# A pre-norm SSM convolution and MLP block on one core: the gate and the norms rewritten, the tail put in order by repeated list schedules

## The chip, the core and the metric

The kernel runs on one NeuronCore of a Trainium2 chip. The core has a matrix engine (TensorE, PE in the profile, with PEld for its weight loads), a vector engine (VectorE, DVE), a scalar engine (ScalarE, ACT), GpSimd (POOL) and a queue engine for transfers (SyncE, SP). Each engine works through its own instructions in the order in which the program issued them and waits on semaphores for the others. The metric is the device time of one execution in microseconds; the profile shows one execution, instruction by instruction.

## What is computed

A sequence of 2048 positions with 512 features, in bfloat16. Part A is a gated long convolution: k is convolved with four taps, multiplied by v, convolved causally over the whole sequence with a per-feature kernel by Fourier transforms, and the result y gates the normalized input. Part B is a normalization, a mixer that shifts features by one or two positions between two matrix products, and an MLP of width 1792.

```python
x = A_q
h = x + _A_ref(_layernorm(x, axis=-1), A_k, A_v, A_shift_k, A_ssm_k, A_ssm_D)   # _A_ref ends in: return q * y
h2 = h + _B_ref(_layernorm(h, axis=-1), B_w1, B_w2, B_w3, B_w4)
...
def _B_ref(x, w1, w2, w3, w4):
    h = _gelu(_layernorm(x, axis=-1) @ w1)
    c = D // 4
    g0 = jnp.pad(h[:, :, 0*c:1*c], ((0, 0), (1, 0), (0, 0)))[:, :S, :]
    ...
    hs = jnp.concatenate([g0, g1, g2, g3], axis=-1) @ w2
    x1 = x + hs
    h2 = _gelu(_layernorm(x1, axis=-1) @ w3) @ w4
    return x1 + h2
```

So h is normalized twice in a row: once to make the input of part B, hn, and that once more ahead of w1. Both are a scale and a shift of h by row.

## The kernel before

The 2048 positions are kept as 16 blocks of 128 rows (position 16p + b lies in partition p of block b), each 128 x 512. The program has three parts.

*The forward transforms* (lines 171 to 414) load k, v, q and the convolution kernel, make tables, transform both factors, and collect mean and variance of each row of q (qstat, lines 361 to 364). qnorm (line 366) turns these into qrs = 1/std and qnm = -mean/std.

*The inverse stage* (lines 418 to 451) loops over 16 frequency blocks. fwd (line 418) does the last transform step on TensorE (step2, line 340, which reads tables in rf), copies it on ScalarE, and forms two products with the kernel's spectrum on VectorE (lines 423 and 424). inv (line 428) transforms back, evacuates PSUM on ScalarE or VectorE by a running count of load (evac, line 282), and stores the block through an SP transfer into wv (line 438), a re-layout that the last transform step reads. Beside the second half of this loop GpSimd computes qn = (q-mean)/std for the 16 blocks (line 450). The loop's end, line 452, is followed by the loads of w1 and w2 on GpSimd's queue (lines 465 and 466, into rf) and of w3 and w4 on SP's (467 and 468).

*The tail* (lines 471 to 705) is written as tasks: each has a name, engines it may run on with a price in microseconds, a function that issues its instructions, tasks it depends on, a buffer pool it takes a slot of, and a task whose buffer it is the last to read. Plan.emit (line 54) makes a list schedule: among all tasks that could run it takes the one with the earliest start, ties going to the longest path behind it (tail), then issues all in order of start. This fixes the order on every engine. The tasks are, for a block b or a pair p of blocks:

- I: the last inverse step for four blocks (32 matmuls, line 503), into four of six PSUM slots ("mm").
- Y: ScalarE copies y to bfloat16 (yb). H, on VectorE: y times qn, plus q gives h; mean and variance of h (hsum, lines 521 to 524).
- rr, on GpSimd: scales and shifts of both normalizations of a pair, with a power of -1/2 (hnorm, lines 530 to 541; line 528 is the power).
- hb: h scaled for w1, on ScalarE or VectorE (lines 548, 550). N, on GpSimd: hn = normalized h (line 556).
- LT and TE: transposes on TensorE (line 563) and copies out of PSUM (lines 483, 485). W: product with w1 for a pair (line 577). U: gelu on ScalarE (line 583).
- X: product with w2 on shifted blocks (line 602); it needs the gelus of the block's neighbours up to two blocks away. S, on VectorE: x1 = X + hn and its statistics (lines 611 to 613).
- r1, on GpSimd: 1/std of x1 (lines 619 and 528). lb: x1 normalized, on VectorE (line 626). L and E: transposes and copies. R, on GpSimd: the residual x1 + h (line 632).
- For four groups of four blocks, M: product with w3 (14 tasks of four matmuls, line 639), G: gelu (line 645), O: product with w4 (four tasks of 14 matmuls, line 654), Z: add the residual and store (lines 662 and 663).

The first group is blocks 2 to 5, since blocks 0 and 1 come last in the mixer's order. M of group g waits for O of group g - 2. In the profile of the page a name such as rd or rc is a large buffer that several stages share.

Of the kernel before, what the change touches and what calls it, by code (L numbers as in the profile page):

```python
# [3 lines left out]

# [6 lines left out]
P = 128  # L11
S = 2048
D = 512
F = 1792
NB = S // P
DC = D // P
FC = F // P
L = 2 * S
# [15 lines left out]
class Plan:  # L34
# [4 lines left out]

    LAT = 0.2  # L40

    def __init__(self, pools):
        self.pools, self.t = pools, []

    def add(self, opts, fn, deps=(), take=None, drop=None, rank=0.0):
        t = dict(opts=opts, fn=fn, deps=[d for d in deps if d is not None], take=take, drop=drop, rank=rank, n=len(self.t),
                 left=0, out=[], done=None)
        if drop is not None:
            t["deps"] = t["deps"] + [drop]
            drop["left"] += 1  # L50
        self.t.append(t)
        return t

    def emit(self):
        for t in self.t:
            for d in t["deps"]:
                d["out"].append(t)
        for t in reversed(self.t):
            t["tail"] = t["rank"] + min(t["opts"].values()) + max((o["tail"] + self.LAT for o in t["out"]), default=0.0)
        held = {p: [] for p in self.pools}  # L60
        free = {e: 0.0 for t in self.t for e in t["opts"]}
        wait, order = list(self.t), []
        while wait:
            best = None
            for t in wait:
                if any(d["done"] is None for d in t["deps"]):
                    continue
                at = max((d["done"] + (0.0 if t["opts"].keys() == {d["eng"]} else self.LAT) for d in t["deps"]), default=0.0)
                if t["take"]:
                    h, k = held[t["take"]], self.pools[t["take"]]  # L70
                    if len(h) >= k:
                        if h[-k]["free"] is None:
                            continue
                        at = max(at, h[-k]["free"] + self.LAT)
                for e, c in t["opts"].items():
                    key = (max(at, free[e]), -t["tail"], c, t["n"])
                    if best is None or key < best[0]:
                        best = key, t, e, c
            (at, *_), t, e, c = best
            t["eng"], t["done"], t["free"] = e, at + c, None  # L80
            free[e] = at + c
            if t["take"]:
                held[t["take"]].append(t)
# [648 lines left out]
```

## Time and profile before

| | |
|---|---|
| Median of three runs | 277.77 us (275.23 to 278.82) |
| The profiled execution | 275.51 us, of it 273.7 us span |
| Mean granted TensorE clock | 0.961 |
| HBM traffic | 11.02 MB read, 2.10 MB written |
| Forward transforms, up to about | 76 us |
| Inverse stage | 76 to 110 us |
| Tail | 110 to 273.7 us |

The span is the time from the first to the last instruction recorded; the execution's own time has 1.8 us more around it. A group row of the profile gives line, engine, operation, output <- input, shape and count, then total busy time and the mean of one in nanoseconds, then the idle time just before these instructions and what ended it. A timeline row gives start, length, engine, line. The chain of waits follows the work back from the last instruction, at each step to what released it.

### The profile page before, as it was taken

How to read it: one execution, taken by the hardware profiler on the slowest of the kernel's cores; microseconds unless marked ns; L12 is line 12 of the kernel's file. 1: busy time of each engine (PE TensorE's matmuls, PEld its weight loads, DVE VectorE, ACT ScalarE, POOL GpSimd, SP SyncE). 2: the span in 40 equal slices, each digit the busy share in tenths (PEclk: the TensorE clock that was granted, in tenths of full speed). 3: DMA queues.
4: the chain of work that ended last, by engine and by line, in shares of the span. 5: the costliest groups of instructions: out<-in, count | busy, mean ns of one | idle time of the engine just before them, and what ended most of it. 6: DMA issues, size and time to landing. Idle time of an engine off the chain costs nothing.

```text
span 273.7 us, 4566 instructions
## 1 busy us (share of the span) xinstructions
PE 234.7 (86%) x1791; PEld 118.1 (43%) x1803; DVE 158.8 (58%) x296; ACT 145.2 (53%) x207; POOL 89.1 (33%) x148
## 2 busy tenths in 40 slices
PE   8666959999399976739878988999999989999994
PEld 4522835664132321214664654444444454444441
DVE  7986736689568996699996999920122240002222
ACT  3628245978679973468983444666300066660000
POOL 4503000000500599688999795840000000000000
PEclk9999997999779999795999999999999999999999
DMA  7999983033303433990000000000011100000111
GB/s 246 251 293 366 377 312 156 2 156 153 154 2 134 175 147 142 357 353 2 2 0 0 2 1 0 2 0 0 0 41 58 38 19 2 0 0 19 54 44 38
DMA packets 18791, 28.08 MB, mean 103 GB/s; under 512 B 10065, under 2 KB 13906, under 8 KB 17234
## 3 DMA queue, kind: packets, MB, share of 16 engines
q1 hardware_dynamic: 17952, 26.74, 28.0%
q0 software_dynamic: 288, 1.05, 0.9%
q8 instruction: 14, 0.23, 0.4%
q10 hardware_dynamic: 530, 0.01, 0.1%
q14 instruction: 7, 0.06, 0.1%
HBM read 11.02 MB, written 2.10 MB: 48 GB/s over the span
## 4 chain that ended last, share of the span: by engine, by line
PE 50%; DVE 23%; POOL 11%; DMA 6%; issue 4%; ACT 4%; SPq 2%; ACTq 0%; DVEq 0%; POOLq 0%
PE mm L654 18%; PE mm L639 17%; POOL rd L556 4%; PE pk L354 4%; DVE st L612 3%; POOL rr L528 3%; DMA rd<-rc 3%; DVE q_sb L611 3%; DVE vst L290 2%; DMA q_sb<-in_A_q_dram 2%; SPq L301 2%; DVE rt L263 2%; PE psg L344 2%; DVE pr L423 2%; PE psk L344 2%
## 5 line engine op out<-in xcount | busy, mean ns | idle before, releaser
L662 DVE TENSOR_TENSOR ob<-mm,rd 128x512 bf16<-128x512 f32 x16 | 11.1, 692 | 76.6 <-PE mm L654 76.6
L639 PE MATMUL mm<-rc,rb 128*128 128x512 bf16 x219 | 48.7, 379 | 1.3 <-DVE q_sb L611 1.0
L654 PE MATMUL mm<-rt,ra 128*128 128x512 bf16 x220 | 48.5, 379 | 0.2
L645 ACT ACTIVATE ra<-mm 128x512 bf16<-128x512 f32 x56 | 33.4, 597 | 19.5 <-PE mm L639 19.5
L639 PEld LDWEIGHTS <-rb 128*128 128x128 bf16 x224 | 21.8, 98 | 27.4 <-issue 1.8
L654 PEld LDWEIGHTS <-ra 128*128 128x128 bf16 x224 | 21.9, 98 | 26.4
L483 ACT COPY rc<-ptx 128x512 bf16<-128x512 bf16 x28 | 15.4, 589 | 32.0 <-PE ptx L563 31.8
L450 POOL TENSOR_SCALAR rd<-q_sb,qrs,qnm 128x512 bf16<-128x512 bf16 x16 | 18.8, 1188 | 18.0 <-DVE pr L424 18.0
L354 PE MATMUL pk<-diag,rb 128*128 128x128 bf16 x256 | 19.0, 232 | 3.0 <-DVE xk L357 2.9
L354 PEld LDWEIGHTS <-rb 128*128 128x128 bf16 x256 | 17.6, 150 | 7.4 <-issue 6.1
L563 PE MATMUL ptx<-ident,hb 128*128 128x128 bf16 x128 | 12.1, 224 | 8.6 <-ACT hb L548 5.1
L632 POOL TENSOR_TENSOR rd<-q_sb,rd 128x512 bf16<-128x512 bf16 x16 | 18.3, 1158 | 1.2 <-DVE q_sb L611 1.2
L577 PE MATMUL mm<-rc,rf 128*128 128x256 bf16 x128 | 16.0, 280 | 0.6 <-ACT rb L583 0.4
L287 ACT CAST asb<-psk 128x1024 bf16<-128x1024 f32 x16 | 16.1, 1030 | 0.5 <-ACT asb L287 0.4
L602 PE MATMUL mm<-rf,rb 128*128 128x512 bf16 x61 | 15.2, 380 | 1.4 <-ACT rb L583 1.0
L503 PE MATMUL mm<-ra,f_71 32*128 32x512 bf16 x128 | 12.3, 490 | 2.9 <-DMA ra<-vst 1.9
L563 PEld LDWEIGHTS <-hb 128*128 128x128 bf16 x128 | 8.7, 99 | 13.7 <-ACT hb L548 6.5
L367 POOL TENSOR_SCALAR qrs<-qmv 128x16 f32<-128x16 f32 x1 | 0.2, 204 | 43.8 <-DVE qmv L363 43.8
L357 DVE TENSOR_TENSOR xk<-pk,rb 128x512 bf16<-128x512 f32 x16 | 10.9, 681 | 5.5 <-PE pk L354 5.5
L577 PEld LDWEIGHTS <-rf 128*128 128x128 bf16 x128 | 12.5, 100 | 3.3 <-issue 1.7
L362 DVE BATCH_NORM_STATS2 qst<-q_sb 128x6 f32<-128x512 bf16 x16 | 10.9, 680 | 5.1 <-DMA q_sb<-in_A_q_dram 5.1
L344 PE MATMUL psg<-rd,rf 128*64 128x512 bf16 x64 | 10.3, 418 | 4.1 <-ACT rd L287 4.0
(213 smaller groups left out, 375.4 us busy)
## 6 DMA issues: line engine op xcount, KB each, us to landing
rd<-rc SPq DMA_DIRECT2D x16, 256.0 KB, 5.0
rc<-ra SPq DMA_DIRECT2D x16, 256.0 KB, 2.4
ra<-vst SPq DMA_DIRECT2D x16, 256.0 KB, 2.4
ra<-in_A_ssm_k_dram SPq DMA_DIRECT2D x4, 512.0 KB, 5.1
rb<-in_A_v_dram SPq DMA_DIRECT2D x2, 1024.0 KB, 8.3
q_sb<-in_A_q_dram SPq DMA_DIRECT2D x2, 1024.0 KB, 6.7
out_dram<-ob SPq DMA_DIRECT2D x16, 128.0 KB, 1.8
rb<-in_B_w_dram SPq DMA_DIRECT2D x1, 1792.0 KB, 7.7
```

The source lines that it names most:

```text
L287: nc.scalar.copy(o, i)
L344: nc.tensor.matmul(ps[64 * t:64 * t + 64, r, :], lhsT=ftab[:, kh, r, t, :], rhs=z[:, kh, t, :], start=True, stop=True)
L354: nc.tensor.matmul(pk[:, c * P:(c + 1) * P], lhsT=kT[:, c, 16 + b - j:KW - 16 + b - j + 1:16], rhs=diag[:, c, j, :], start=(j == 0), stop= ...
L450: nc.gpsimd.tensor_scalar(out=qn[:, b, :], in0=q_sb[:, b, :], scalar1=qrs[:, b:b + 1], scalar2=qnm[:, b:b + 1], op0=MUL, op1=ADD)
L483: nc.scalar.copy(o, i)
L563: nc.tensor.transpose(pt[:, c, :], tl[key][:, c * P:(c + 1) * P], ident[:])
L577: nc.tensor.matmul(pw_[:, j * 256:(j + 1) * 256], lhsT=w1_sb[:, k, m * P:(m + 1) * P], rhs=hnT[:, k, p * 256:(p + 1) * 256], start=(k == 0 ...
L602: nc.tensor.matmul(px[:], lhsT=shifted(m, b), rhs=w2_sb[:, m, :], start=(m == 0), stop=(m == DC - 1))
L632: nc.gpsimd.tensor_tensor(out=xh1[:, b, :], in0=x1[:, b, :], in1=h_sb[:, b, :], op=ADD)
L639: nc.tensor.matmul(pg[:], lhsT=w3_sb[:, k, fc * P:(fc + 1) * P], rhs=lnT[:, k, g * 512:(g + 1) * 512], start=(k == 0), stop=(k == DC - 1))
L645: nc.scalar.activation(gbuf[:, g % 2, fc, :], tl["g", g, fc][:], ACT.Gelu_apprx_tanh)
L654: nc.tensor.matmul(po[:], lhsT=gbuf[:, g % 2, fc, i * P:(i + 1) * P], rhs=w4_sb[:, fc, :], start=(fc == 0), stop=(fc == FC - 1))
```

## The change

The new kernel computes the same function.

- Plan is rewritten. `forward` is a list schedule as before (earliest start, then a priority, where the engine is chosen by earliest finish). `backward` takes the engines of a forward schedule and schedules the tasks from the end, one after another on each engine, which gives each a latest start; these are the priorities of the next forward schedule. `solve` does this 40 times, with random disturbances every sixth time, and keeps the order whose planned end is earliest. A task may take several slots at once (`many`), and the slots are freed one by one (`part`).
- qn, qnm and their GpSimd passes are gone. y is gated as h = (q - mean) * (1 + y/std): ScalarE makes z = 1 + y*qrs in float32 (`gate`), VectorE makes (q - mean) * z. The stored h lacks the row mean of q, which the residual adds back. (The two normalizations do not see a constant added to a row.)
- hn is no longer computed. hb, the normalized input of w1, is kept for all 16 blocks in rd, and x1 is hb * cr + X, where cr, the ratio of the two scales (tasks `cr`), turns the second normalization back into the first.
- The variance-plus-epsilon and the negated mean move from GpSimd to VectorE (`uw`, `ux`); GpSimd keeps the powers and the small products. The scale-and-shift passes hb and lb are both in the form multiply, add, and may run on VectorE, GpSimd or ScalarE.
- The residual R moves from GpSimd to VectorE and now also waits for the last M of its group.
- A dummy gelu after the inverse stage loads ScalarE's table there. The pools yb (4) and hb (5) go; z (4) and lb (6) come. Prices in the tasks are changed, and M, O and E get ranks for the first forward schedule.

```diff
+    def forward(self, prio):
...
+            for n in ready:
+                t, at0 = ts[n], 0.0
...
+                at0 = {e: max([at0, free[e]] + [done[d] + (0.0 if eng[d] == e else self.LAT) for d in t["deps"]]) for e in t["opts"]}
+                e = min(at0, key=lambda e: (at0[e] + t["opts"][e], t["opts"][e]))
+                key = (at0[e], -prio[n], n)
+                if best is None or key < best[0]:
...
+            (at, *_), n, e, c = best
+            t = ts[n]
+            done[n], eng[n] = at + c, e
             free[e] = at + c
...
+            order.append((at, n))
+        return max(done.values()), order, done, eng
+
+    def backward(self, done, eng):
...
+        while ready:
+            best = None
+            for n in ready:
+                e = eng[n]
+                at = max([free[e]] + [left[o] + (0.0 if eng[o] == e else self.LAT) for o in ts[n]["out"]])
+                key = (at, -done[n], n)
+                if best is None or key < best[0]:
+                    best = key, n, e
+            (at, *_), n, e = best
+            left[n] = free[e] = at + ts[n]["opts"][e]
+            ready.remove(n)
...
+        return left
...
+    def solve(self):
+        tail, best, rnd = {}, None, random.Random(1)
+        for t in reversed(self.t):
+            tail[t["n"]] = t["rank"] + min(t["opts"].values()) + max((tail[o] + self.LAT for o in t["out"]), default=0.0)
+        prio = top = tail
+        for i in range(self.rounds):
+            r = self.forward(prio)
+            if r is not None and (best is None or r[0] < best[0]):
+                best, top = r, prio
+            if r is None or i % 6 == 5:
+                prio = {n: p + rnd.gauss(0.0, 3.0) for n, p in top.items()}
+            else:
+                prio = self.backward(r[2], r[3])
+        return best
+
+    def emit(self):
+        best = self.solve()
+        for _, n in sorted(best[1]):
+            self.t[n]["fn"](best[3][n])
+        return best[0]
...
-        nc.gpsimd.tensor_tensor(out=qnm[:], in0=qmv[:, :, 0], in1=qrs[:], op=MUL)
-        nc.gpsimd.tensor_scalar(out=qnm[:], in0=qnm[:], scalar1=-1.0, scalar2=0.0, op0=MUL, op1=ADD)
...
-    qn = view(rd, NB * D, NB * D, "p (b d) -> p b d", b=NB)
...
-        if i >= NH // 2 + 1:
-            for b in range(2 * (i - NH // 2 - 1), min(NB, 2 * (i - NH // 2))):
-                nc.gpsimd.tensor_scalar(out=qn[:, b, :], in0=q_sb[:, b, :], scalar1=qrs[:, b:b + 1], scalar2=qnm[:, b:b + 1],
-                                        op0=MUL, op1=ADD)
...
+    nc.scalar.activation(dum[:], negpi[:], ACT.Gelu_apprx_tanh)
...
-    hn, xh1, x1 = qn, qn, q_sb
+    hbm = view(rd, NB * D, NB * D, "p (b d) -> p b d", b=NB)
+    xh1, x1 = hbm, q_sb
...
     nc.gpsimd.memset(h1T[:, :, :, XW - 1:XW], 0.0)
-    plan = Plan({"mm": 6, "pt": 2, "yb": 4, "hb": 5})
...
-    def ycopy(b):
-        def f(e):
-            yb = tl["yb", b] = lnp.tile([P, D], BF16, name="yb", tag="yb", bufs=4)
-            copy(e, yb[:], tl["y", b][:])
-        return f
+    def inv1(bl):
...
+    def gate(b):
+        def f(e):
+            z = tl["z", b] = lnp.tile([P, D], F32, name="z", tag="z", bufs=4)
+            nc.scalar.activation(z[:], tl["y", b][:], ACT.Identity, bias=1.0, scale=qrs[:, b:b + 1])
+        return f
+
+    def stats(name, b, src):
+        mv = pair(name, b // 2, 2, 2, bufs=8)
+        st = stp.tile([P, 6], F32, name="st", tag="st")
+        nc.vector.bn_stats(st[:], src)
+        nc.vector.bn_aggr(mv[:, b % 2, :], st[:])
...
     def hsum(b):
         def f(e):
...
-            nc.vector.tensor_tensor(out=ty[:], in0=tl["yb", b][:], in1=qn[:, b, :], op=MUL)
-            nc.vector.tensor_tensor(out=h_sb[:, b, :], in0=ty[:], in1=q_sb[:, b, :], op=ADD)
-            nc.vector.bn_stats(st[:], h_sb[:, b, :])
-            nc.vector.bn_aggr(mv[:, i, :], st[:])
-        return f
-
-    def power(dst, n):
-        nc.gpsimd.tensor_tensor(out=dst, in0=dst, in1=mhalf[:, 0:n], op=OP.pow)
+            nc.vector.scalar_tensor_tensor(out=h_sb[:, b, :], in0=q_sb[:, b, :], scalar=qmv[:, b, 0:1], in1=tl["z", b][:],
+                                           op0=SUB, op1=MUL)
+            stats("hv", b, h_sb[:, b, :])
+        return f
...
+    def negmean(p, n, mv):
+        nm = pair(n, p, 2, bufs=8)
+        nc.vector.tensor_scalar(out=nm[:], in0=mv[:, :, 0], scalar1=-1.0, scalar2=None, op0=MUL)
+
...
+    def hvar(p):
...
+            uw = pair("uw", p, 2, 2, bufs=8)
+            for a, (m_, e_) in enumerate(((1.0, EPS), (1.0 + EPS, EPS * EPS))):
+                nc.vector.tensor_scalar(out=uw[:, a, :], in0=tl["hv", p][:, :, 1], scalar1=m_, scalar2=e_, op0=MUL, op1=ADD)
+            negmean(p, "hm", tl["hv", p])
+        return f
...
     def hnorm(p):
         def f(e):
...
-            for a, (m_, e_) in ((1, (1.0 + 1e-5, 1e-10)), (0, (1.0, 1e-5))):
-                nc.gpsimd.tensor_scalar(out=rr[:, a, :], in0=mv[:, :, 1], scalar1=m_, scalar2=e_, op0=MUL, op1=ADD)
-            power(rr[:].rearrange("p a i -> p (a i)"), 4)
-            for a in range(2):
-                nc.gpsimd.tensor_tensor(out=nm[:, a, :], in0=mv[:, :, 0], in1=rr[:, a, :], op=MUL)
-            nc.gpsimd.tensor_scalar(out=nm[:], in0=nm[:], scalar1=-1.0, scalar2=0.0, op0=MUL, op1=ADD)
-        return f
+            uw, rr, nm = tl["uw", p], pair("rr", p, 2, 2, bufs=8), tl["hm", p]
+            power(rr[:].rearrange("p a i -> p (a i)"), uw[:].rearrange("p a i -> p (a i)"), 4)
+            nc.gpsimd.tensor_tensor(out=nm[:], in0=nm[:], in1=rr[:, 1, :], op=MUL)
+        return f
...
+    def hback(p):
...
+            uw, rr, cr = tl["uw", p], tl["rr", p], pair("cr", p, 2, bufs=8)
+            nc.gpsimd.tensor_tensor(out=cr[:], in0=uw[:, 1, :], in1=rr[:, 1, :], op=MUL)
+            nc.gpsimd.tensor_tensor(out=cr[:], in0=cr[:], in1=rr[:, 0, :], op=MUL)
+        return f
...
+    def scaled(e, o, i, sc, bi):
+        if e == "A":
+            nc.scalar.activation(o, i, ACT.Identity, bias=bi, scale=sc)
+        else:
+            (nc.gpsimd if e == "G" else nc.vector).tensor_scalar(out=o, in0=i, scalar1=sc, scalar2=bi, op0=MUL, op1=ADD)
...
     def hbf(b):
         def f(e):
...
-    def hnf(b):
...
-            nc.gpsimd.tensor_scalar(out=hn[:, b, :], in0=h_sb[:, b, :], scalar1=sc, scalar2=bi, op0=MUL, op1=ADD)
+            tl["hb", b] = hbm[:, b, :]
+            scaled(e, hbm[:, b, :], h_sb[:, b, :], tl["rr", b // 2][:, 1, b % 2:b % 2 + 1], tl["hm", b // 2][:, b % 2:b % 2 + 1])
...
     def x1sum(b):
         def f(e):
...
-            nc.vector.tensor_tensor(out=x1[:, b, :], in0=tl["x", b][:], in1=hn[:, b, :], op=ADD)
-            nc.vector.bn_stats(st[:], x1[:, b, :])
-            nc.vector.bn_aggr(tl["mv2", b // 2][:, i, :], st[:])
+            nc.vector.scalar_tensor_tensor(out=x1[:, b, :], in0=hbm[:, b, :], scalar=tl["cr", b // 2][:, b % 2:b % 2 + 1],
+                                           in1=tl["x", b][:], op0=MUL, op1=ADD)
+            stats("xv", b, x1[:, b, :])
...
+    def xvar(p):
...
+            nc.vector.tensor_scalar(out=pair("r1", p, 2)[:], in0=tl["xv", p][:, :, 1], scalar1=1.0, scalar2=EPS, op0=MUL, op1=ADD)
+            negmean(p, "xm", tl["xv", p])
...
     def x1norm(p):
         def f(e):
...
+            power(r1[:], r1[:], 2)
+            nc.gpsimd.tensor_tensor(out=nm[:], in0=nm[:], in1=r1[:], op=MUL)
...
     def lbf(b):
         def f(e):
...
-            nc.vector.tensor_scalar(out=hb[:], in0=x1[:, b, :], scalar1=tl["mv2", b // 2][:, b % 2, 0:1],
-                                    scalar2=tl["r1", b // 2][:, b % 2:b % 2 + 1], op0=SUB, op1=MUL)
...
+            scaled(e, lb[:], x1[:, b, :], tl["r1", b // 2][:, b % 2:b % 2 + 1], tl["xm", b // 2][:, b % 2:b % 2 + 1])
...
     def resid(b):
         def f(e):
-            nc.gpsimd.tensor_tensor(out=xh1[:, b, :], in0=x1[:, b, :], in1=h_sb[:, b, :], op=ADD)
+            nc.vector.scalar_tensor_tensor(out=xh1[:, b, :], in0=x1[:, b, :], scalar=qmv[:, b, 0:1], in1=h_sb[:, b, :],
+                                           op0=ADD, op1=ADD)
...
-            for i in range(4):
-                task(("I", b + i), {"PE": 2.2 * (i == 3)}, inv1(b + i), [("I", b + i - 1)] if b + i else [], take="mm")
-        task(("Y", b), {"A": 0.6}, ycopy(b), [("I", b | 3)], take="yb", drop=("I", b))
-        task(("H", b), {"V": 1.75}, hsum(b), drop=("Y", b))
+            task(("I", b // 4), {"PE": 2.45}, inv1(b // 4), take="mm", many=4)
+        task(("Y", b), {"A": 0.72}, gate(b), take="z", drop=("I", b // 4), part=b % 4)
+        task(("H", b), {"V": 1.6}, hsum(b), drop=("Y", b))
...
-            task(("rr", p), {"G": 2.0}, hnorm(p), [("H", b - 1), ("H", b)])
+            task(("uw", p), {"V": 0.24}, hvar(p), [("H", b - 1), ("H", b)])
+            task(("rr", p), {"G": 1.35}, hnorm(p), [("uw", p)])
+            task(("cr", p), {"G": 0.55}, hback(p), [("rr", p)])
...
-                task(("hb", c), {"A": 0.68, "V": 0.42}, hbf(c), [("rr", p)], take="hb")
...
+                task(("hb", c), {"V": 0.42, "G": 0.92, "A": 0.8}, hbf(c), [("rr", p)])
...
-            for c in (b - 1, b):
-                task(("N", c), {"G": 0.9}, hnf(c), [("rr", p)])
...
-        task(("S", b), {"V": 1.6}, x1sum(b), [("N", b)], drop=("X", b))
+        task(("S", b), {"V": 1.6}, x1sum(b), [("cr", b // 2)], drop=("X", b))
...
-            task(("r1", p), {"G": 1.2}, x1norm(p), [("S", b - 1), ("S", b)])
+            task(("ux", p), {"V": 0.17}, xvar(p), [("S", b - 1), ("S", b)])
+            task(("r1", p), {"G": 1.05}, x1norm(p), [("ux", p)])
...
-                task(("lb", c), {"V": 0.42}, lbf(c), [("r1", p)], take="hb")
+                task(("lb", c), {"V": 0.42, "G": 0.92, "A": 0.8}, lbf(c), [("r1", p)], take="lb")
...
-                task(("R", c), {"G": 1.2}, resid(c), [("S", c)])
+                task(("E", c), {"A": 0.6, "V": 0.42}, tcopy(("lb", c), lnT, order.index(c)), drop=("L", c),
+                     rank=400.0 - 20.0 * (order.index(c) // 2))
...
-                 take="mm")
...
+                 take="mm", rank=100.0 - 20.0 * g)
...
+        for b in bs:
+            task(("R", b), {"V": 0.76}, resid(b), [("S", b), ("M", g, FC - 1)])
...
```

153 lines of the change are left out of this document (70 added, 83 removed).

## The prediction

> **What bounds the kernel now.** I read the page first, then each stage by windows, then the chain of work, then groups and timeline.
>
> ```profile
> span 273.7 us, 4566 instructions
> PE 234.7 (86%) x1791; PEld 118.1 (43%) x1803; DVE 158.8 (58%) x296; ACT 145.2 (53%) x207; POOL 89.1 (33%) x148
> ```
>
> TensorE is busiest, but that share is a mean over unlike stages. The windows cut the planned tail (lines 471 to 705) at its turning points. After the two times and the length come PE, PEld, DVE, ACT and POOL busy, granted clock, DMA share and GB/s.
>
> ```profile
> 110.38:141.20 30.82, 23.32 (x220) 13.50 (x221) 27.81 (x61) 23.70 (x42) 26.05 (x54) 0.83 0.41 152
> 141.20:172.02 30.82, 26.55 (x179) 15.43 (x181) 27.61 (x56) 15.21 (x29) 24.74 (x38) 1.00 0.00 1
> 172.02:218.80 46.78, 46.57 (x215) 21.28 (x219) 12.52 (x23) 15.66 (x27) 8.27 (x10) 1.00 0.06 20
> 218.80:221.50 2.70, 1.93 (x25) 1.44 (x23) 2.44 (x6) 1.64 (x3) 0.00 (x0) 1.00 0.14 49
> 221.50:270.36 48.86, 48.53 (x227) 22.16 (x230) 5.70 (x11) 17.20 (x29) 0.00 (x0) 1.00 0.06 19
> sum 159.98, PE 146.90 PEld 73.80 DVE 76.09 ACT 73.41 POOL 59.06; mean PE 29.38 PEld 14.76 DVE 15.22 ACT 14.68 POOL 11.81
> ```
>
> From 172.02 TensorE is full. In the 61.6 us before that, VectorE is busy 55.4 and GpSimd 50.8, TensorE only 49.9. Over the tail TensorE idles 159.98 - 146.90 = 13.1 us, 11.8 of it before 172.02. That idle time is what another order can win. The chain (start, length, what) says who holds TensorE back:
>
> ```profile
> 118.25 1.69 POOL rd L556 x2
> ...
> 122.53 1.69 POOL rd L556 x2
> ...
> 145.31 1.02 POOL rr L528
> ...
> 171.40 0.59 DVE q_sb L611
> 172.02 7.50 PE mm L639 x34
> ```
>
> Up to 147 GpSimd's norm work sets the pace, 122.53 - 118.25 = 4.28 us for a pair of blocks; then VectorE's x1 sums (line 611) hold it to 172. The first feed-forward matmuls (M, line 639) come at the end of all that, though the first group of them needs only four x1 blocks.
>
> **The change, part by part.**
>
> *Before the tail.* The sixteen (q-mean)/std passes of line 450 leave GpSimd. Groups of the products in the inverse stage from 76 to 92.2, without those passes, and from 92.2 to 107.5, beside them; the last row is that second window:
>
> ```profile
> L423 DVE TENSOR_TENSOR pr<-asb,rd 128x1024 bf16<-128x1024 bf16 x9 | 6.2, 688 | 2.8 <-ACT asb L287 2.8
> ...
> L423 DVE TENSOR_TENSOR pr<-asb,rd 128x1024 bf16<-128x1024 bf16 x7 | 5.9, 846 | 0.1
> L424 DVE TENSOR_TENSOR pr<-asb,rd 128x1024 bf16<-128x1024 bf16 x7 | 5.6, 798 | 0.0
> ...
> 92.20:107.50 15.30, 11.50 (x88) 3.50 (x90) 14.54 (x18) 11.04 (x12) 15.25 (x12) 1.00 0.36 135
> ```
>
> VectorE is the bound there (14.54 of 15.30), and its products grew by 7 x (0.846 - 0.688) + 7 x (0.798 - 0.688) = 1.9 us. This comes back: **-1.9 us** on the path (other end 0, if ScalarE's evacuations become the bound at once). The two small operations that made qnm go too; nothing waits for GpSimd there, so they are worth nothing.
>
> *Weights.* On GpSimd's queue the w1 and w2 loads stood behind line 450.
>
> ```profile
> 101.25 0.62 PE L344 MATMUL psk<-rc,rf 128*64 128x512 bf16 x4
> ...
> 110.99 1.02 POOL L465 DMA_DIRECT2D rf<-in_B_w_dram  x1
> ...
> ra<-vst SPq DMA_DIRECT2D x8, 256.0 KB, 2.4
> ...
> rf<-in_B_w_dram POOLq DMA_DIRECT2D x2, 512.0 KB, 7.5
> ```
>
> They now wait only for rf's last reader, at 101.9, and go out 9 us sooner, beside the last of the inverse stage's stores, the last of which the tail waits for. Ends: 0, and +2.4, that store taking twice its time. I take 0, since the loads are issued some 4 us ahead of it. Landing sooner wins nothing: before, they had landed by 119.5 and W began at 128. On SP's queue the w3 and w4 loads and the output stores keep their places.
>
> *Gate and h.* Before: ScalarE copy, VectorE multiply, add, statistics. Now ScalarE makes 1 + y/std in float32, one VectorE scalar_tensor_tensor makes h, then statistics.
>
> ```profile
> L523 DVE BATCH_NORM_STATS2 st<-rd 128x6 f32<-128x512 bf16 x16 | 11.1, 695 | 0.6
> ...
> L611 DVE TENSOR_TENSOR q_sb<-mm,rd 128x512 bf16<-128x512 f32 x16 | 10.6, 661 | 0.0
> L522 DVE TENSOR_TENSOR rd<-ty,q_sb 128x512 bf16<-128x512 bf16 x16 | 8.9, 556 | 0.5
> L521 DVE TENSOR_TENSOR ty<-yb,rd 128x512 bf16<-128x512 bf16 x16 | 7.5, 470 | 3.9 <-ACT yb L483 3.9
> ...
> L524 DVE BATCH_NORM_AGGREGATE mv<-st 128x2 f32<-128x6 f32 x16 | 2.9, 182 | 0.7
> ...
> L241 DVE SCALAR_TENSOR_TENSOR u1k<-u1k,pf,u1p x1: 279/279/279, 3.5 to 3.5; 128x64 int32<-128x64 int32 x1
> ...
> L256 DVE SCALAR_TENSOR_TENSOR u0k<-u0k,pf,u0p x1: 346/346/346, 5.1 to 5.1; 128x128 int32<-128x128 int32 x1
> ```
>
> H was 0.470 + 0.556 + 0.695 + 0.182 = 1.90 us. No row has the new form at this size. From 64 to 128 elements it grows by 67 ns, so at 512 it is 346 + 6 x 67 = 748 ns; the lower end is 661 (line 611, a two-input form with one float32 input). I take 0.75, being the same operation: H is then 1.63, and VectorE's work falls by **0.27 x 16 = 4.3 us**. The x1 sum takes the same form, 0.66 to 0.75: **+1.4** at most. [...]
>
> The gate on ScalarE lies between 0.60 (line 645) and 0.81 (line 548, two pointer scalars), against 0.59 for the copy:
>
> ```profile
> L645 ACT ACTIVATE ra<-mm 128x512 bf16<-128x512 f32 x56 | 33.4, 597 | 19.5 <-PE mm L639 19.5
> ...
> L548 ACT ACTIVATE hb<-rd,nm,rr x10: 797/812/824, 118.2 to 138.9; 128x512 bf16<-128x512 bf16 x10
> ...
> 111.06 2.05 ACT L483 CAST yb<-mm 128x512 bf16<-128x512 f32 x4 [5.80 <-PE mm L503]
> ...
> 128.76 1.28 ACT L583 ACT_TABLE_LOAD   x1
> ```
>
> That is at most 16 x 0.22 = 3.5 us on an engine busy 38.9 of 61.6, hidden; without that cover the first gate alone lies on the path, +0.22. The Gelu table load, 1.28 us, moves into the 5.80 us in which ScalarE waits for the transform: hidden both times, so nothing; at best 1.28 of ScalarE at 128.76.
>
> *Norm work.* GpSimd loses the sixteen hn passes (line 556) and the sixteen residual sums (line 632) and hands its smallest multiply-adds to VectorE, 8 x 3 and 8 x 2 operations of two elements a partition or so. Ends 0 and 0.18 each (line 524); I take 0.10, since they follow each other with no wait: **+4 us** of VectorE.
>
> ```profile
> L556 POOL TENSOR_SCALAR rd<-rd,rr,nm 128x512 bf16<-128x512 bf16 x16 | 13.3, 841 | 0.3
> ...
> L539 POOL TENSOR_TENSOR nm<-mv,rr 128x2 f32<-128x2 f32 x16 | 3.8, 257 | 0.6
> ```
>
> For a pair GpSimd keeps the power (1.02) and three products of 0.26: 1.8 us in place of 4.28. The pace passes to VectorE: 2 x 1.63 + 0.3 = 3.6 us a pair. The residual sums on VectorE are 16 x 0.75 = 12 us; each waits for the last M of its group, where VectorE works 12.5 of 46.8 and 5.7 of 48.9 us, so they are hidden; without cover the last output waits 0.75. The hb blocks live in rd and no longer wait for one of five buffers; the trace shows no such wait, so nothing.
>
> *The order.* The old list ranks a task by the longest path behind it, which put all H ahead of the x1 sums. The new one ranks by latest starts from a backward pass that counts TensorE as one queue, and behind the first M stand 98 us of M and O (172.02 to 270.36). So group 0's x1 sums are wanted early. I place the first M with these rows besides:
>
> ```profile
> L483 ACT COPY rc<-ptx x28: 565/586/610, 120.1 to 222.9; 128x512 bf16<-128x512 bf16 x28
> ...
> 130.99 1.91 PE L577 MATMUL mm<-rc,rf 128*128 128x256 bf16 x16
> ...
> 162.89 1.03 PE L602 MATMUL mm<-rf,rb 128*128 128x512 bf16 x4
> ```
>
> The first gate comes 1.9 before 111.06, at 109.2; first H at 109.9; four pairs, 4 x 3.6, end at 124.3. Then norm 1.4, hb 0.8, transposes and copies 1.3, W 1.9, gelu 0.6, two X 2.1: 132.4; two x1 sums with statistics 3.2, norm 1.4, and lb, transpose and copy 2: **139**. Before, it is 169 to 172. From 108.5 to 139 TensorE can have done some 26 us (all of inv1, five pairs of transposes and W, four X), so it idles 4.5; behind that, M and O of groups 0 and 1 fill what the late sums leave, and I allow 2.5 for waits. Idle 7.0 in place of 13.1: **-6.1** (ends: 3 us idle, -10.1; and no gain, 0).
>
> **Sum.** -1.9 - 6.1 = -8.0. What VectorE saves and gains is inside the 139 and is not added again. The profiled execution took 275.51 us (span 273.7 and 1.8 around it), so 267.5 by it. The median of the runs shown, 277.77, lies 2.3 above; from it **269.8**.
>
> **Rivals.**
>
> *M does not come forward.* Both lists choose by earliest start first and priority second; where VectorE is saturated this may keep H ahead. Then GpSimd's pace of 4.28 becomes VectorE's 3.6 and some 0.4 of stretch, 8 x 0.28 = 2.2 better, and the x1 sums lose 1.4: -1.9 - 0.8, **275.1**. For it: VectorE is busy 55.4 of 61.6 us and its sum barely falls. Against: group 0 needs only half of the H work.
>
> *Slower: wide GpSimd passes stretch VectorE, and TensorE waits in line.* hb and lb may now go to GpSimd. Beside wide GpSimd work the rows read:
>
> ```profile
> 119.33 0.88 DVE L522 TENSOR_TENSOR rd<-ty,q_sb 128x512 bf16<-128x512 bf16 x1
> ...
> L626 DVE TENSOR_SCALAR hb<-q_sb,mv_2185,r_2231 x2: 407/408/408, 161.4 to 161.7; 128x512 bf16<-128x512 bf16 x2
> L626 DVE TENSOR_SCALAR hb<-q_sb,mv_2225,r_2286 x2: 1237/1258/1280, 162.1 to 163.3; 128x512 bf16<-128x512 bf16 x2
> ```
>
> A sum is stretched by 0.88 - 0.56 = 0.32 or more, a scaled pass by 0.85. If sixteen H (5.1) and ten scaled passes or copies (8.5) are hit, VectorE is 13.6 us longer, and M tasks interleaved in TensorE's strict order wait with it: 269.8 + 13.6 = **283.4**. From 8 us of stretch nothing is won, from 13.5 it is slower by 2%. Against it: 13.3 us of line 556 leave GpSimd, and half of VectorE's sums read PSUM. [...]
>
> **How the numbers follow.** Forecast 0.62 (264 to 272), first rival 0.28 (272 to 279), slower 0.10 (279 to 286). The range reaches down to the best idle, 277.8 - 1.9 - 10.1 = 265.8, less the 2.3 between profile and median, 263.5, and up into the first rival, 276.5. Two per cent, about what a measurement of this kernel can tell from no change, is 272.2 and 283.3. A little of the forecast lies above 272.2, half of the slower rival below 283.3: faster 0.60, same 0.34, slower 0.06.
>
> **What would show it.** Right: lines 423 and 424 at 0.69 throughout and inv1 ending 1.9 sooner; H at 1.6 us; the first M between 139 and 146; TensorE idle 7 us over the tail. Wrong: the first M past 160, the new form of H past 0.9, or TensorE waiting for VectorE between M matmuls.

## The result and the profile after

The changed kernel takes 267.12 us in the median of four runs (266.27 to 268.60), against 277.12 for the kernel before (the three runs of the table ahead and one more). The ratio is 0.9647, with a 95% interval of 0.9566 to 0.9728: 10.0 us less, where 8.0 was forecast. Ratios here and below leave out executions that took over 1.5% longer than the fastest of the same kernel.

The profiled execution is the slowest of the four (268.60 us). Its page and its windows over the tail, cut at the first gate, the first M and the last product, with the same cuts in the kernel before (first copy of y, first M, last product); columns as in the prediction (the first M of the changed kernel is recorded from 156.9 on, overlapping the matmuls before it):

```profile
span 266.8 us, 4530 instructions
PE 231.9 (87%) x1803; PEld 119.0 (45%) x1803; DVE 161.9 (61%) x323; ACT 143.3 (54%) x202; POOL 54.1 (20%) x101
```

```profile
112.54:140.00 27.46, 20.17 (x206) 12.88 (x204) 25.34 (x65) 19.43 (x34) 20.01 (x33) 0.88 0.32 120
140.00:157.03 17.03, 15.63 (x124) 10.22 (x125) 16.28 (x39) 12.33 (x22) 10.86 (x20) 1.00 0.01 1
157.03:183.12 26.09, 26.09 (x166) 14.02 (x164) 20.59 (x50) 16.23 (x28) 9.30 (x15) 1.00 0.00 1
183.12:263.45 80.33, 80.29 (x372) 36.22 (x370) 18.89 (x30) 22.20 (x38) 0.00 (x0) 1.00 0.08 25
112.54:263.45 150.91, 142.18 (x864) 73.34 (x861) 81.11 (x181) 70.19 (x120) 40.16 (x67) 0.98 0.10 36
```

```profile
111.06:140.00 28.94, 21.63 (x204) 12.55 (x202) 26.68 (x59) 22.50 (x39) 24.30 (x51) 0.82 0.42 158
140.00:168.98 28.98, 25.51 (x181) 15.39 (x182) 25.84 (x52) 15.36 (x29) 22.93 (x37) 1.00 0.00 1
168.98:270.36 101.38, 99.08 (x472) 45.64 (x479) 23.57 (x45) 35.55 (x60) 11.15 (x14) 1.00 0.06 20
111.06:270.36 159.30, 146.22 (x852) 73.58 (x861) 76.09 (x154) 73.41 (x127) 58.38 (x100) 0.97 0.11 42
```

From first gate to last product the tail went from 159.3 to 150.9 us, 8.4 less. Both spend their first 28 us alike, with TensorE idle 7.3 us. The kernel before idles another 3.5 us before its first M at 168.98 and 2.3 after it; the changed one 1.4 before its first M at 157.03 and nothing worth naming after. The rest of the difference is TensorE's busy time itself, 4.0 us less. Most of that is the inverse step, whose matmuls ran at a higher granted clock here (0.88 in the first window against 0.82; over the first 64 of the 96 below 1.00 against 0.76, over the other 32 1.00 against 0.50); the clock differs between executions of one program (its mean over the span was 0.953 to 0.961 in the four of the changed kernel), so whether this is gain is taken up below. Its 96 recorded matmuls in the first of those windows, line 503 before and line 549 after:

```profile
111.06:140.00 28.94, 9.76 (x96) 3.30 (x93) 0.82 0.42 158
```

```profile
112.54:140.00 27.46, 6.49 (x96) 2.54 (x93) 0.88 0.32 120
```

The chain of waits of the changed kernel (start, length, what) in the middle of the tail:

```profile
128.87 0.70 DVE st L566
...
130.57 1.53 POOL rd L611 x2
...
137.44 1.41 POOL rr L591
...
139.15 0.41 DVE rd L611
...
141.85 0.65 DVE rd L571
142.52 0.70 DVE st L566
...
143.47 0.24 DVE uw L586 x2
143.78 0.66 DVE q_sb L667
144.46 0.70 DVE st L566
...
152.73 0.40 PE ptx L623 x4
153.13 0.86 PE mm L662 x4
...
157.03 0.86 PE mm L702 x4
...
190.89 24.17 PE mm L717 x112
215.06 18.99 PE mm L702 x88
```

GpSimd's work carries it from 129.8 to 139.1 only (powers, small products and the wide passes of line 611); before, it did so from 115.6 to 147, nearly without a break. Otherwise VectorE carries it from the first gate on (lines 571 and 667 are the new forms of h and of the x1 sum), until TensorE takes over at 152.7, and from then on it is TensorE's own queue, M between X and transposes. Before, VectorE held it up to 172.

What lies ahead of the changed code differs by chance: the inverse stage's first product starts at 80.7 us here and at 78.5 in the profile before, and between 76.8 and 80.6 in the profiles of the runs below. So the spans of single profiles differ by less or more than the medians, and stages are compared from their own beginnings.

### The profile page after: what moved, and what is told of

Its sections match the earlier page's. It is cut to its first block, busy times and chain, and to the rows that moved or that the text cites. A ratio compares the mean times of both kernels' runs of the same rounds, so it can differ in the third digit from the quotient of the medians.

```text
span 266.8 us, 4530 instructions
## 1 busy us (share of the span) xinstructions
PE 231.9 (87%) x1803; PEld 119.0 (45%) x1803; DVE 161.9 (61%) x323; ACT 143.3 (54%) x202; POOL 54.1 (20%) x101
## 4 chain that ended last, share of the span: by engine, by line
PE 57%; DVE 24%; DMA 6%; ACT 5%; POOL 4%; issue 2%; ACTq 0%; POOLq 0%
PE mm L717 18%; PE mm L702 18%; DVE st L566 4%; PE pk L406 4%; PE mm L662 3%; DVE rd L571 3%; DMA q_sb<-in_A_q_dram 3%; DMA rd<-rc 2%; DVE rt L315 2%; PE psg L396 2%; DVE vst L342 2%; ACT rc L339 2%; PE psk L396 2%; PE psva L484 2%; DVE pr L474 1%
## 5 line engine op out<-in xcount | busy, mean ns | idle before, releaser
L702 PE MATMUL mm<-rc,rb 128*128 128x512 bf16 x224 | 50.8, 379 | 0.0
L406 PE MATMUL pk<-diag,rb 128*128 128x128 bf16 x256 | 19.8, 238 | 4.4 <-DVE xk L409 4.3
L637 PE MATMUL mm<-rc,rf 128*128 128x256 bf16 x128 | 17.8, 295 | 0.0
L662 PE MATMUL mm<-rf,rb 128*128 128x512 bf16 x64 | 16.2, 380 | 1.0 <-ACT rb L643 0.9
L571 DVE SCALAR_TENSOR_TENSOR rd<-q_sb,qmv,z 128x512 bf16<-128x512 bf16 x16 | 12.7, 792 | 4.6 <-ACT z L560 4.6
L560 ACT ACTIVATE z<-mm,qrs 128x512 f32<-128x512 f32 x16 | 10.6, 697 | 7.4 <-PE mm L549 5.7
L667 DVE SCALAR_TENSOR_TENSOR q_sb<-rd,cr,mm 128x512 bf16<-128x512 bf16 x16 | 11.7, 733 | 3.7 <-PE mm L662 3.7
L396 PEld LDWEIGHTS <-rf 128*64 128x64 bf16 x128 | 5.7, 115 | 17.2 <-issue 16.2
L473 DVE TENSOR_TENSOR pr<-asb,rd 128x1024 bf16<-128x1024 bf16 x16 | 11.0, 687 | 3.5 <-ACT asb L339 3.5
L339 ACT CAST rd<-psg 128x1024 bf16<-128x1024 f32 x13 | 13.0, 1028 | 0.0
```

The costliest lines, as they stand in the source:

```text
L339: nc.scalar.copy(o, i)
L396: nc.tensor.matmul(ps[64 * t:64 * t + 64, r, :], lhsT=ftab[:, kh, r, t, :], rhs=z[:, kh, t, :], start=True, stop=True)
L406: nc.tensor.matmul(pk[:, c * P:(c + 1) * P], lhsT=kT[:, c, 16 + b - j:KW - 16 + b - j + 1:16], rhs=diag[:, c, j, :], start=(j == 0), stop= ...
L571: nc.vector.scalar_tensor_tensor(out=h_sb[:, b, :], in0=q_sb[:, b, :], scalar=qmv[:, b, 0:1], in1=tl["z", b][:], op0=SUB, op1=MUL)
L637: nc.tensor.matmul(pw_[:, j * 256:(j + 1) * 256], lhsT=w1_sb[:, k, m * P:(m + 1) * P], rhs=hnT[:, k, p * 256:(p + 1) * 256], start=(k == 0 ...
L662: nc.tensor.matmul(px[:], lhsT=shifted(m, b), rhs=w2_sb[:, m, :], start=(m == 0), stop=(m == DC - 1))
```

## The experiments

Twelve runs. The table gives each ratio to the kernel before with its interval, then, from the one profiled execution of each: the length of the inverse stage (first product of fwd to first gate), and, in us behind the first gate, the last H, the first x1 sum, the first M and the end of the last product (the tail; the windows above end 0.1 us behind it in the kernel before).

| run | ratio (interval) | inverse stage | last H | first x1 sum | first M | tail |
|---|---|---|---|---|---|---|
| before | 1 | 32.6 | 30.8 | 37.6 | 57.9 | 159.2 |
| changed | 0.9647 (0.9566 to 0.9728) | 31.9 | 29.2 | 31.1 | 44.3 | 150.9 |
| x10_after_again (the same) | 0.9679 (0.9629 to 0.9730) | 31.3 | 29.2 | 31.1 | 44.3 | 150.8 |
| x1_old_rule | 1.0033 (0.9995 to 1.0072) | 32.0 | 29.3 | 41.4 | 61.8 | 162.3 |
| x9_old_rule_merged | 0.9868 (0.9772 to 0.9963) | 31.8 | 28.4 | 34.9 | 55.0 | 155.4 |
| x2_old_math | 1.0022 (0.9972 to 1.0072) | 32.6 | 31.9 | 33.6 | 54.2 | 160.7 |
| x3_q_passes | 0.9708 (0.9654 to 0.9763) | 32.6 | 29.2 | 31.1 | 44.3 | 150.8 |
| x5_no_wide_gps | 0.9631 (0.9542 to 0.9721) | 31.7 | 28.4 | 30.0 | 44.5 | 151.0 |
| x6_r_gps | 0.9712 (0.9630 to 0.9793) | 31.6 | 30.0 | 32.0 | 44.5 | 151.8 |
| x8_w_on_sp | 0.9651 (0.9565 to 0.9736) | 31.3 | 29.3 | 31.2 | 44.4 | 150.9 |
| x11_hn_gps | 0.9706 (0.9653 to 0.9759) | 31.7 | 30.5 | 32.9 | 47.4 | 153.0 |
| x12_h_longer | 0.9717 (0.9667 to 0.9767) | 31.8 | 39.0 | 27.6 | 44.2 | 153.0 |
| x4_s_first | 0.9578 (0.9510 to 0.9645) | 31.3 | 46.3 | 24.5 | 37.2 | 149.0 |
| x13_s_first_again (the same) | 0.9570 (0.9516 to 0.9625) | 31.7 | 46.3 | 24.5 | 37.2 | 149.0 |

The tail's length is the sharper measure. The changed kernel's is 150.8 to 150.9 in both its profiles and in two runs whose tail is the same program (x3_q_passes, x8_w_on_sp), while the whole times of these four profiled executions run from 265.98 to 268.60 us.

### The order taken away

```diff
-    def __init__(self, pools, rounds=40):
+    def __init__(self, pools, rounds=1):
...
-                e = min(at0, key=lambda e: (at0[e] + t["opts"][e], t["opts"][e]))
-                key = (at0[e], -prio[n], n)
+                for e, c in t["opts"].items():
+                    key = (at0[e], -prio[n], c, n)
```

The ranks of M, O and E go too.

> The changed kernel with its new arithmetic, but put in order by one forward schedule with the old rule (earliest start, then the longest path behind a task, no ranks, no repeats). If the order is what shortened the tail by 8 us, most of that comes back: 273 to 276 us, and TensorE idles 13 us or more between the first gate and the last product, as before the change. If the lighter work of VectorE and GpSimd did it, whatever the order, it stays at 267 to 269 us with 9 us idle.

Measured: no gain at all is left, ratio 1.0033, and the tail is longer than before the change, with 16.9 us of TensorE idle time. The median, 277.63 us, lies above both answers. The waits of this run, engine and line, what it waited for, then total, times and longest:

```profile
POOL rr L591 <- DVE uw L586: 27.8, 1, 27.8
...
PE ptx L623 <- DVE hv L567: 9.1, 1, 9.1
```

The small operations that feed GpSimd's power are now tasks in VectorE's queue. The old rule put twelve of the sixteen H ahead of the first of them (the next expectation says all sixteen). GpSimd stood 27.8 us in one piece: its first power comes 20.2 us behind the first gate, where it comes at 6.1 in the changed kernel. TensorE then stood 9.1 us in one piece. This is more than the gain being due to the order: the new arithmetic has a hazard that the old rule runs into. The next run takes that hazard away and leaves the rule.

```diff
-        task(("H", b), {"V": 1.6}, hsum(b), drop=("Y", b))
+        def both(b=b):
+            def f(e):
+                hsum(b)(e)
+                if b % 2:
+                    hvar(b // 2)(e)
+            return f
+        task(("H", b), {"V": 1.6 + 0.24 * (b % 2)}, both(), [("H", b - 1)] if b % 2 else [], drop=("Y", b))
```

The same is done for the x1 sum and its `xvar`.

> As the run with the new arithmetic and the old rule (277.6 us), but the small operations that feed GpSimd's power are issued in the same task as the statistics, as the old kernel had them within one task, instead of being tasks of their own on VectorE. In the earlier run GpSimd waited 27.8 us for them and TensorE 9.1 us in one piece, since the old rule put all sixteen H ahead of them. If that queueing alone undid the gain, this run gives 268 to 272 us: the arithmetic is worth most of it and the repeated schedules mend a hazard that the change itself brought in. If the old rule is bad for the tail whatever the tasks are, 273 to 277.

Measured: 0.9868, a median of 271.95 us, on the upper edge of the first answer; the tail is 155.4. So of the 8.3 us by which the tail shrank, the lighter arithmetic gives 3.8 under the old rule, and the new schedule 4.5 more. That is the new schedule as a whole: the choice of the engine by earliest finish, the ranks, the small operations as tasks of their own and the repeated rounds were not tried one by one.

### The arithmetic taken away

The old kernel with the new `Plan`, its statistics tiles made by whichever of a pair comes first.

> The old kernel with its old arithmetic (qn passes, hn on GpSimd, residual sums on GpSimd), but ordered by the new repeated schedules. If the order alone did it: 269 to 271 us, the rest being the inverse stage's 1.5 us that the qn passes cost. If GpSimd's 4.28 us for a pair of blocks is the real limit, no order can go around it and it stays at 274 to 277 us, with GpSimd's norm work still on the chain of waits.

Measured: 1.0022, no gain (the median of all ten executions is 278.47); the second answer. In its chain GpSimd's power for a pair comes every 4.3 to 4.5 us, as before the change:

```profile
129.69 1.02 POOL rr L581
...
134.22 1.02 POOL rr L581
...
138.71 1.02 POOL rr L581
```

The new order needs the new arithmetic. Two runs asked which part of it, by putting a load back into the changed kernel, on GpSimd and on VectorE.

```diff
...
+                task(("N", c), {"G": 0.9}, extra(c), [("rr", p)])
...
-        task(("S", b), {"V": 1.6}, x1sum(b), [("cr", b // 2)], drop=("X", b))
+        task(("S", b), {"V": 1.6}, x1sum(b), [("cr", b // 2), ("N", b)], drop=("X", b))
```

> The changed kernel with sixteen wide GpSimd passes put back after the norm work of each pair (a scale and shift of h into a scratch buffer that nothing reads; the plan lets the x1 sum wait for them, as hn did). The old arithmetic under the new order stayed at 278, and either GpSimd's load or VectorE's longer H could be why. If GpSimd's load is the reason, this run gives 272 to 276, with the wide passes between the powers on the chain of waits. If VectorE's H is, it stays at 266 to 268.

```diff
+            t = lnp.tile([P, D], BF16, name="scr", tag="scr", bufs=2)
+            nc.vector.tensor_tensor(out=t[:], in0=q_sb[:, b, :], in1=q_sb[:, b, :], op=MUL)
             nc.vector.scalar_tensor_tensor(out=h_sb[:, b, :], in0=q_sb[:, b, :], scalar=qmv[:, b, 0:1], in1=tl["z", b][:],
...
-        task(("H", b), {"V": 1.6}, hsum(b), drop=("Y", b))
+        task(("H", b), {"V": 2.02}, hsum(b), drop=("Y", b))
```

> The changed kernel with one more 128 x 512 product on VectorE in each H (into a scratch buffer, read by nothing), so that H is about as long as the old one (2.1 us against 1.9). If VectorE's pace in the front is what the new order lives on, 16 x 0.42 = 6.7 us more VectorE work comes back nearly in full: 271 to 274. If GpSimd's load was the limit and VectorE has room, 266 to 268.

The control beside these two is the changed kernel itself, without an edit:

> The changed kernel as it is, for comparison with the other three on the same chip: 0.965 of the kernel before, 266 to 267.5 us.

Measured: tails of 153.0 in both, 2.2 us longer, and whole times that the intervals can't part from the control's. In neither does the load come back nearly in full: 12.4 us of wide passes on GpSimd, and 6.6 us on VectorE, cost 2.2 us each.

```profile
L610 POOL TENSOR_SCALAR scr<-rd,rr,hm 128x512 bf16<-128x512 bf16 x16 | 12.4, 780 | 0.0
```

```profile
L572 DVE TENSOR_TENSOR scr<-q_sb 128x512 bf16<-128x512 bf16 x16 | 6.6, 410 | 2.6 <-DMA ra<-vst 2.6
```

The schedule moves around either: with the longer H it begins the x1 sums at 27.6 and lets the last H come at 39.0. Both expectations named one limit, and both were wrong in that.

### The residual sums back on GpSimd

```diff
-            task(("R", b), {"V": 0.76}, resid(b), [("S", b), ("M", g, FC - 1)])
+            task(("R", b), {"G": 1.2}, resid(b), [("S", b), ("M", g, FC - 1)])
```

> The changed kernel with the sixteen residual sums put back on GpSimd (one tensor_tensor each; q's row mean is then left out of the output, so the values differ from the reference by it). The forecast hid them on VectorE behind M and O at no cost, so moving them back should change nothing: 266.5 to 267.7. If their place on GpSimd was part of what held the front back, 268 to 270, with H or the norm work beside them stretched.

(The operation is the old kernel's, without q's row mean.) Measured: tail 151.8, 1.0 us longer; the median of 268.26 us lies in the second answer, but the ratio, 0.9712, is not parted from the control's. With the two runs above, 2.2 + 2.2 + 1.0 = 5.4 of the 10 us between the tails of x2_old_math and of the changed kernel are accounted for, if the three add up, which no run shows. The rest is open: the old kernel's small norm operations on GpSimd, its hb and lb in five shared buffers, lb on VectorE alone and the missing ranks were not tried one by one.

### The passes over q

```diff
+        if i >= NH // 2 + 1:
+            for b in range(2 * (i - NH // 2 - 1), min(NB, 2 * (i - NH // 2))):
+                nc.gpsimd.tensor_scalar(out=qn[:, b, :], in0=q_sb[:, b, :], scalar1=qrs[:, b:b + 1], scalar2=qrs[:, b:b + 1],
+                                        op0=MUL, op1=ADD)
```

> The changed kernel with sixteen scale-and-shift passes over q put back on GpSimd in the inverse stage (their output is overwritten later and used by nothing). The forecast's first term says that they stretch VectorE's products from 0.69 to about 0.8 us there and cost 1.9 us: 268.5 to 269. The first trace after the change shows the inverse stage shorter by 1.5 up to its last evacuation, but the first gate only 0.8 earlier: by that 268. If ScalarE's evacuations were the bound anyway, 267.1 and no difference.

Measured: the inverse stage is 32.6 us long in all three profiles with the passes and 31.3 to 32.0 in all others. The products of the stage, in the changed kernel and in this run (VectorE groups, then the passes):

```profile
L473 DVE TENSOR_TENSOR pr<-asb,rd 128x1024 bf16<-128x1024 bf16 x16 | 11.0, 687 | 3.5 <-ACT asb L339 3.5
L474 DVE TENSOR_TENSOR pr<-asb,rd 128x1024 bf16<-128x1024 bf16 x16 | 11.0, 685 | 0.0
```

```profile
L473 DVE TENSOR_TENSOR pr<-asb,rd 128x1024 bf16<-128x1024 bf16 x16 | 12.1, 756 | 2.9 <-ACT asb L339 2.8
L474 DVE TENSOR_TENSOR pr<-asb,rd 128x1024 bf16<-128x1024 bf16 x16 | 11.7, 734 | 0.0
...
L500 POOL TENSOR_SCALAR rd<-q_sb,qrs 128x512 bf16<-128x512 bf16 x16 | 18.7, 1185 | 18.6 <-DVE pr L474 18.6
```

The passes lengthen the products by 1.8 us (12.1 + 11.7 against 22.0), and about 1 us of it reaches the first gate. The whole time went up by 0.6% in the ratio, 0.3% against the control, which the intervals don't settle. The tail, with 2.1 us less idle time and 2.1 us more busy time on TensorE, is as long as without them.

### Wide passes off GpSimd, and the weights on another queue

```diff
-                task(("hb", c), {"V": 0.42, "G": 0.92, "A": 0.8}, hbf(c), [("rr", p)])
+                task(("hb", c), {"V": 0.42, "A": 0.8}, hbf(c), [("rr", p)])
```

The same edit is made to lb.

> The changed kernel where hb and lb may run on VectorE or ScalarE only (the schedule is made anew). The slower rival said that GpSimd's wide passes stretch VectorE by up to 13.6 us; the trace after the change shows the sixteen H at 0.79 us in the mean against 0.72 undisturbed, 1.1 us in all. If the stretch is that small and GpSimd's help is needed, taking it away costs: 268 to 272 us. If contention is the larger part, this run is faster than 266.

```diff
-    nc.gpsimd.dma_start(w1_sb, B_w1.rearrange("(k p) o -> p k o", p=P))
-    nc.gpsimd.dma_start(w2_sb, B_w2.rearrange("(k p) o -> p k o", p=P))
+    nc.sync.dma_start(w1_sb, B_w1.rearrange("(k p) o -> p k o", p=P))
+    nc.sync.dma_start(w2_sb, B_w2.rearrange("(k p) o -> p k o", p=P))
```

> The changed kernel with the loads of w1 and w2 moved from GpSimd's queue to SP's, behind the last store of the inverse stage. In the trace after the change these loads ran from 104 to 109 us beside the last stores, one of which took 3.46 us in place of 2.42. If that delays the last inverse step, the first gate comes 0.5 to 1 us sooner and the time falls to 266 to 266.6, as long as w1 lands before W wants it some 12 us later. If the stores are not on the path, 267.1 as before; if w1 now lands late, 268 to 270.

Measured: neither changes anything that can be told (0.9631 and 0.9651, tails 151.0 and 150.9). The new form of h, in the changed kernel and in the run without wide GpSimd passes:

```profile
L571 DVE SCALAR_TENSOR_TENSOR rd<-q_sb,qmv,z 128x512 bf16<-128x512 bf16 x16 | 12.7, 792 | 4.6 <-ACT z L560 4.6
```

```profile
L571 DVE SCALAR_TENSOR_TENSOR rd<-q_sb,qmv,z 128x512 bf16<-128x512 bf16 x16 | 11.7, 734 | 4.4 <-ACT z L560 4.4
```

The stretch is small, 16 x 0.058 = 0.9 us, and nearly all of it is in two of the sixteen: in the changed kernel two took 1.20 us, each begun 0.1 us after a wide pass on GpSimd, and the other fourteen 0.72 to 0.75. The first expectation had asked for GpSimd's help to be worth 1 us or more; it isn't.

### The first M brought forward

```diff
...
+    for b in range(12, NB):
+        T["H", b]["deps"].append(T["S", 5]["n"])
+        T["S", 5]["out"].append(T["H", b]["n"])
     plan.emit()
```

(The lines left out only let `solve` walk a plan in which a task waits for one added later.)

> The changed kernel where blocks 12 to 15 may start their h only after the x1 sum of block 5, in the plan alone. This brings the first feed-forward product forward, to some 40 us behind the first gate in place of 45, as the forecast had wanted it (30). If TensorE's idle time is what is left once the first M is late, it falls by 2 us or more: 263 to 265. If TensorE has W and X to do from 140 us on whatever M's place, and its idle time is the start-up ahead of that, nothing is won: 266 to 269.

> The run in which blocks 12 to 15 wait for the x1 sum of block 5, unchanged, against the changed kernel on the same chip. In the first run it was at 0.958 of the kernel before against 0.965 for the changed kernel, with the tail 1.9 us shorter and 1.7 us less TensorE idle time. If that is real, it is 1 to 2.5 us faster than the changed kernel here too; if it was the chip or the run, both lie within 0.3%.

Measured: 0.9578 and 0.9570, medians of 265.50 and 264.22 us, against 266.98 for the changed kernel beside the second. The first lies between its two answers. Both tails are 149.0. This version beats both kernels; against the changed one it is 1.1% faster by the two ratios, with intervals that just fail to meet (0.9625 and 0.9629). Its windows, up to the first M and after it:

```profile
109.98:147.20 37.22, 30.70 (x288) 19.15 (x286) 34.24 (x87) 25.24 (x43) 20.25 (x35) 0.91 0.24 91
147.20:258.95 111.75, 111.36 (x577) 53.51 (x575) 50.21 (x105) 41.14 (x71) 16.25 (x27) 1.00 0.06 18
sum 148.97, PE 142.05 PEld 72.66 DVE 84.46 ACT 66.38 POOL 36.50; mean PE 71.03 PEld 36.33 DVE 42.23 ACT 33.19 POOL 18.25
```

TensorE idles 6.9 us, 6.5 of it before the first M at 37.2, and 0.4 in the 111.8 us after. So an order with x1 sums ahead of the late H, and the first M 7 us sooner, is worth 1.9 us of tail, though the schedule's own search did not find it. The earlier x1 sums alone are not enough: in x12_h_longer they begin at 27.6, and the first M still comes at 44.2.

## Why the prediction came out right

The direction, the size (8.0 against 10.0) and the range held; the single terms held less well. That the total came so near is in part luck: the step behind its largest term, -6.1, failed, that term came to -4.4 in the profiled execution, and TensorE's busy time, which the forecast put at nothing, fell by 4.0.

- **The inverse stage, -1.9.** The mechanism is shown: with the passes the products are stretched (to 0.76 and 0.73 us in the mean in x3_q_passes), without them they take 0.69 throughout. Up to the end of the stage's last evacuation it measured 1.4 (29.4 to 28.0 us behind the first product); the first gate came 0.7 sooner in this profile and about 1.0 in the mean of the table. The step that leads up to the gate is the first inverse step, and the clock granted to it differs from one execution to the next: 0.50 in the changed kernel's profile, 1.00 in the kernel before's, and 1.00 in x10_after_again, the same program as the changed kernel, where the first gate came 1.3 sooner (31.3 against 32.6). From the first inverse matmul on, the three windows in that order:

```profile
109.00:111.20 2.20, 2.11 (x21) 0.85 (x25) 0.00 (x0) 0.00 (x0) 0.00 (x0) 0.50 0.80 215
```

```profile
107.40:110.38 2.98, 1.83 (x24) 0.45 (x25) 0.48 (x1) 0.00 (x0) 2.98 (x5) 1.00 0.84 240
```

```profile
106.56:109.98 3.42, 2.60 (x34) 0.65 (x35) 0.17 (x1) 0.00 (x1) 0.00 (x0) 1.00 0.80 220
```

- **The weights, 0.** Right: put on another queue, they cost and gain nothing.
- **The new form, 0.75.** It took 0.72 to 0.75 undisturbed, and the x1 sum 0.73; the gate took 0.70, inside 0.60 to 0.81. H came to 0.792 + 0.695 + 0.182 = 1.67 for the forecast's 1.63. The small operations began 0.07 to 0.1 apart where nothing stood between, as assumed.
- **The first M at 139.** This step failed. It was to follow the first gate by 30 us and follows it by 44.3. The order did not put group 0's x1 sums ahead of the late H: the last H starts at 29.2 and the first x1 sum at 31.1. Why the search kept this order stays open. The pace of a pair was nearly right, 3.8 us for 3.6 (28.5 us from the first H to the sixteenth, fifteen steps).
- **Idle 7.0 in place of 13.1.** It is 8.7, so this term measured -4.4 in place of -6.1. It survived the failed step because TensorE was short of work mostly up to about 140; from there W and X fill all but 1.4 us of its time up to the first M. The other 4.0 us are TensorE's busy time; 3.3 of them (9.76 to 6.49) are the inverse step's matmuls at a higher granted clock, 1.00 in place of 0.76 for the first 64 of the 96 and of 0.50 for the rest. That these 3.3 us shorten the tail is not shown: in x3_q_passes, with the same tail program, TensorE is busy 2.1 us longer and idle 2.1 us less (6.5), and the tail is as long. So how the 8.4 us divide between idle and busy time depends on the execution, and by that one the idle term would be -6.6; their sum does not.
- **The rival in which M does not come forward** named the right order of events, all H before all x1 sums, and priced it at 275.1. What it missed is that the sums start as soon as the last H is done (31.1, not 37.6), since GpSimd's norm work is no longer behind by then.
- **The slower rival** is refuted. It needs a stretch of 13.6 us, 5.1 of it on H; on H it is 0.9 us, and taking the wide passes off GpSimd gains nothing.

The forecast priced the order by itself (-6.1) and left the lighter arithmetic inside it. The runs show that neither stands alone: under the old rule the new arithmetic loses everything to a queue, or keeps 3.8 of 8.3 us of tail if that queue is avoided; and the new order alone wins nothing.

## What to carry to other kernels

A task split into smaller ones can lose more in an engine's queue than the lighter work saves (here, under the old rule, 6.9 us of tail were lost, 162.3 against 155.4, where 3.8 had been saved); whether it does was decided here by the rule that orders them, so arithmetic and schedule are to be tried together and apart. In this kernel a later start of the bottleneck's main work cost only the time in which the bottleneck had nothing else to do (the first M 7.1 us sooner was worth 1.9 us of tail); read its idle time, by stretches, before pricing a start. Beside a schedule search that repeats, a hand-made constraint or two is worth trying: one, four H that wait for an x1 sum, took 1.9 us more out of the tail than forty rounds had.

## What the runs showed of the hardware

TensorE's clock can be halved in one execution and full in another at the same place of the same program: behind the inverse stage it was 0.50 in the changed kernel's profile and 1.00 in x10_after_again (the windows above), though in the 3 us ahead TensorE was busy 1.20 us in the one and 1.21 in the other. So TensorE's load just ahead does not settle it alone. Where TensorE stood 9.1 us in one piece, in the run with the old rule, the clock was 0.57 over the window around that gap, and 0.50 for 7.5 us of work behind it, from 133.3 to 140.8:

```profile
125.00:140.00 15.00, 5.76 (x37) 4.41 (x38) 13.95 (x47) 9.17 (x14) 8.64 (x13) 0.57 0.00 1
...
133.30:140.80 7.50, 6.55 (x41) 4.96 (x42) 6.72 (x16) 6.16 (x9) 6.95 (x12) 0.50 0.00 1
```

GpSimd's power of 128 x 4 elements took 1.01 us in the mean in the run with the old rule and 1.28 in the changed kernel. There three of the eight took 1.00 to 1.01, and five, begun while VectorE was in the product of an H (line 571), 1.40 to 1.49:

```profile
L591 POOL TENSOR_TENSOR rr<-uw,mhalf 128x4 f32<-128x4 f32 x8 | 10.2, 1278 | 13.7 <-PE mm L549 13.7
```

So the stretch is seen on both sides: beside wide bfloat16 passes on GpSimd two H took 1.20 us in place of 0.72, and beside the product of an H five of GpSimd's powers took 1.40 to 1.49 us in place of 1.01. It is not on the same side each time: in x11_hn_gps three H ran wholly beside wide passes in 0.74 to 0.75 us, and there a GpSimd pass took 1.27 to 1.32 us in place of 0.77. The x1 sums, which read one input from PSUM, took 0.72 beside wide passes in the changed kernel, no more than elsewhere (0.72 to 0.75), and in the kernel before 0.66 to 0.68, beside wide passes and away from them. All this is read from profiles; only the run without wide passes tried a part of it by itself.
